# First tokens as rows turned by TensorE, head loads in one order, and a fixed table of order, engines and buffers in place of a list scheduler

## The chip, the cores and the metric

One core of a Trainium2 chip runs the kernel. The time is device microseconds of one execution, the median of several runs. A profiled execution has in addition a span, from the first to the last recorded instruction, and a trace of every engine. TensorE is called PE in the rows (PEld is its weight load), VectorE DVE, ScalarE ACT, GpSimd POOL; SP issues DMAs.

## The reference, cut to what matters

2048 tokens of width 640, 32 heads of 20. Branch A is a linear attention with learned feature maps, branch B a causal attention inside four segments of 512 tokens with a memory that is carried from segment to segment. A gate per token mixes them.

```python
q, k, v = A heads of x @ wqkv
phi_q = concat(softmax(q @ w_phi), softmax(-q @ w_phi))   # per head; phi_k alike
kv = sum over s of phi_k v ; z = sum over s of phi_k
a = (phi_q @ kv / (phi_q @ z + 1e-6)) @ wo_A
for s in range(4):                                       # branch B, L = 512
    p = softmax(qs @ ks.T * scale + causal mask)
    a_dot = p @ vs
    a_mem = phi(qs) @ M / (phi(qs) @ z + 1e-6)
    o = sigmoid(beta) * a_mem + (1 - sigmoid(beta)) * a_dot
    M += phi(ks).T @ vs ; z += sum phi(ks)
g = sigmoid((x * gate_w).sum(-1))
out = g * a + (1 - g) * (o @ wo_B)
```

## The kernel before, in words

The kernel is a graph of operations. Each method of `GatedMix` calls `op` or `dma` with the engines an operation may run on, a duration, the tiles it reads and writes, and a priority; an operation's place in this list of calls is its index. `schedule` (a list scheduler) then takes operation after operation by assumed durations and priorities: which comes next, which of two engines an evacuation runs on, which buffer of a pool and which PSUM banks a tile takes. `emit` writes one instruction stream per engine in that order, with a wait on a semaphore wherever an operand comes from another engine. On the chip every engine and every DMA queue takes its own stream in order.

PSUM has eight banks, handed out as single banks, pairs, or two pairs for a burst of QK. The exponentials of attention go to a pool `p_exp` of two buffers.

Names: `setup` loads. `x0` to `x3` are DMAs that turn 512 tokens each into `xT` (features on partitions); `stq`, `stk` are the q and k weights of branch B, which VectorE spreads into `WB` in groups of 32 columns; `WvB`, `WvA` the two v weights; `wkT`, `wqT` turned weights of branch A, from which `fuse` makes `WkA`, `WqA`. Segment n of branch B has ten `qkproj` (five chained 512-column matmuls, index 2c for q and 2c+1 for k of chunk c), four `vproj`, then eight steps in the order of GORD. A step (`b_step`) is three QK bursts (numbered 0, 1, 2), five exponentials of 128x1024 on ScalarE, four masks on GpSimd, two halves of PV (12 and 28 matmuls, numbered 0 and 1) and a combination of two VectorE operations. `Mmm`, `Nmm` update and read the memory; `b_out` scales and turns a tile into `oTB` by DMA. Branch A: `pkA`, `vA` for each of 16 token tiles, with a sum, a reciprocal, a product and running sums on VectorE; `kv` per segment; then `pqA`, `Zq`, a trip of the normaliser through DRAM, `U` per tile, turned into `oTA`. `final` adds both branches of one tile in 20 matmuls; its evacuation and the store to `out` follow. An evacuation (`evac`) may run on ScalarE or VectorE.

Before, SP issues x0, wkT, x1, x2, x3, wqT in this order, and ScalarE's queue stq, stk, WvB, WvA. The order of segments on TensorE, counted from one segment's first QK burst to the next, is in the table of the section on the change.

Of the kernel before, what the change touches and what calls it, by code (L numbers as in the profile page):

```python
# [13 lines left out]
D = 640  # L14
# [14 lines left out]
MW = 420 + 21 * 16  # L29

# [70 lines left out]
class Graph:  # L101
# [33 lines left out]
    def schedule(self):  # L135
        free = {s: 0.0 for s in STREAMS}
        bank_occ = [None] * 8
        bank_t = [0.0] * 8
        bank_prev = [()] * 8
        fillers = set()  # L140
        for o in self.ops:
            o.nleft = len(o.deps)
            for d in o.deps:
                d.succ.append(o)
            for t in o.tiles:
                t.left += 1
        ready = {s: [] for s in STREAMS}

        def push(o):
            for e in o.engs:  # L150
                ready[e].append(o)
        for o in self.ops:
            if o.nleft == 0:
                push(o)
        LAT = 0.09

        def dep_time(o, e):
            m = 0.0
            for d in o.deps:
                t = d.end  # L160
                if d.stream == e and e == "pe" and not d.dma:
                    continue
                if d.dma:
                    t = d.end + 0.1
                elif d.stream != e:
                    t += LAT
                else:
                    t += 0.03
                if t > m:
                    m = t  # L170
            return m

        def tile_avail(t, commit=False, rank=0):
            if t.slot is not None:
                return 0.0
            p = t.pool
            if p is None:
                return 0.0
            if isinstance(p, PsumPool):
                n = t.shape  # L180
                if n == 1:
                    best = None
                    for b in range(8):
                        if bank_occ[b] is None:
                            lone = bank_occ[b ^ 1] is None
                            c = (bank_t[b] + (0.3 if lone else 0.0), b)
                            if best is None or c < best:
                                best = c
                    if best is None:
                        return None  # L190
# [16 lines left out]
                if not opts:  # L207
                    return None
# [1034 lines left out]
```

## Time and profile before

| | us |
|---|---|
| median of 3 runs | 404.66 (404.42 to 407.14) |
| profiled execution | 401.42 |
| its span | 399.7 |
| TensorE busy | 313.9 |
| ScalarE busy | 257.3 |
| VectorE busy | 226.3 |
| GpSimd busy | 127.9 |

The profile has a page of totals, views of busy time by stretch, of groups of instructions by line, of instructions in order of time, of who waited for whom, and a chain of waits, followed back from the last instruction, which names at each moment the work that the end depended on. Busy times of different engines overlap. A matmul's recorded duration includes its way through the array, so chained matmuls follow each other faster than that.

### The profile page before, as it was taken

The page shows a single profiled execution, that of the slowest core. Times are in us where ns is not written, and L with a number is a line of the kernel's source. Part 1 is how long each engine was busy: PE and PEld are TensorE (multiplying, and loading weights), DVE is VectorE, ACT ScalarE, POOL GpSimd, SP SyncE. Part 2 cuts the span into 40 slices and gives each one's busy share as a digit, 9 for nine tenths or more (in the row PEclk, how much of TensorE's full clock was granted, in tenths as well). Part 3 has the DMA queues.
Part 4 walks back from the last instruction along what each step waited for, and adds up shares of the span by engine and source line. Part 5 has one row for each costly group of instructions (what it writes and reads, how often), then busy time and mean ns, then how long its engine had stood idle before and what let it go on. Part 6 is the DMA issues. An engine that isn't in the chain of part 4 may idle for free.

```text
span 399.7 us, 8357 instructions
## 1 busy us (share of the span) xinstructions
PE 313.9 (79%) x3594; PEld 180.9 (45%) x3594; DVE 226.3 (57%) x388; ACT 257.3 (64%) x334; POOL 127.9 (32%) x153
## 2 busy tenths in 40 slices
PE   0398796796888696988979689998999669938466
PEld 0144353463464354545326355554655346517233
DVE  3043696977797749658606996532443586126120
ACT  1047877579765855674977876797577864584602
POOL 5000561146535545272520232232322231133400
PEclk9999999899898969989989999999898857975559
DMA  8996800150100301006511526751320543423131
GB/s 184 301 202 115 128 15 16 30 77 2 52 18 2 66 2 31 13 16 195 66 48 28 134 48 150 147 85 46 59 59 16 115 98 80 130 84 36 32 66 66
DMA packets 70933, 30.51 MB, mean 76 GB/s; under 512 B 58961, under 2 KB 68465, under 8 KB 70897
## 3 DMA queue, kind: packets, MB, share of 16 engines
q1 hardware_dynamic: 68176, 26.68, 32.1%
q10 hardware_dynamic: 2624, 3.28, 2.6%
q0 software_dynamic: 96, 0.04, 0.5%
q8 instruction: 28, 0.46, 0.5%
q14 instruction: 9, 0.07, 0.1%
HBM read 10.08 MB, written 7.77 MB: 45 GB/s over the span
## 4 chain that ended last, share of the span: by engine, by line
PE 50%; DVE 25%; ACT 15%; DMA 5%; POOL 2%; issue 2%; POOLq 0%; ACTq 0%
PE ps L1162 9%; PE ps L736 9%; ACT expT L871 9%; PE ps L978 5%; PE ps L912 5%; DVE acc L1032 5%; PE ps L758 4%; DMA xT<-in_A_x_dram 4%; PE ps L1135 3%; PE ps L862 3%; PE ps L1083 3%; ACT expT L890 3%; DVE z L991 3%; DVE oA L1144 2%; PE ps L1163 2%
## 5 line engine op out<-in xcount | busy, mean ns | idle before, releaser
L876 POOL TENSOR_SCALAR_AFFINE_SELECT expT<-expT 128x512 bf16<-128x512 bf16 x128 | 92.5, 725 | 227.3 <-ACT expT L871 180.8
L871 ACT ACTIVATE expT<-ps 128x1024 bf16<-128x1024 f32 x128 | 124.0, 1025 | 30.9 <-PE ps L862 30.7
L736 PE MATMUL ps<-xT,WB 128*128 128x512 bf16 x200 | 51.2, 401 | 19.3 <-DMA xT<-in_A_x_dram 16.8
L912 PE MATMUL ps<-v1B,expT 128*128 128x21 bf16 x1280 | 40.7, 175 | 15.5 <-ACT expT L871 6.5
L912 PEld LDWEIGHTS ps<-v1B,expT 128*128 128x128 bf16 x1280 | 37.8, 98 | 25.5 <-POOL expT L876 8.5
L720 ACT ACTIVATE qkm<-ps 128x512 bf16<-128x512 f32 x31 | 18.4, 597 | 32.8 <-PE ps L736 32.6
L736 PEld LDWEIGHTS ps<-xT,WB 128*128 128x128 bf16 x200 | 19.0, 102 | 42.7 <-issue 22.4
L890 ACT ACTIVATE expT<-ps 128x1024 bf16<-128x1024 f32 x32 | 32.7, 1023 | 8.3 <-PE ps L862 8.2
L862 PE MATMUL ps<-qkm 20*128 20x512 bf16 (+3 forms) x320 | 23.3, 325 | 17.1 <-ACT expT L871 11.4
L1032 DVE TENSOR_TENSOR acc<-acc,E 64x1280 bf16<-64x1280 bf16 x31 | 32.9, 1061 | 5.9 <-POOL E L993 5.1
L993 POOL TENSOR_TENSOR E<-E,z 128x1280 bf16<-128x1280 bf16 x12 | 28.9, 2409 | 15.5 <-DVE z L992 15.5
L720 ACT ACTIVATE out<-ps 128x640 bf16<-128x640 f32 x16 | 11.3, 704 | 33.3 <-PE ps L1163 33.3
L758 PE MATMUL ps<-WvB,xT 128*128 128x512 bf16 x80 | 27.0, 419 | 4.0 <-DVE mo L952 1.2
L1162 PE MATMUL ps<-Wo,oTA 128*128 128x512 bf16 x80 | 24.9, 397 | 5.5 <-DMA oTB<-oB 4.4
L991 DVE TENSOR_REDUCE z<-E 128x64 f32<-128x1280 bf16 x16 | 23.7, 1479 | 9.3 <-ACT E L985 9.2
L985 ACT ACTIVATE E<-ps 128x640 bf16<-128x640 f32 x32 | 22.6, 707 | 9.1 <-PE ps L979 8.8
L978 PE MATMUL ps<-WkA,xT 128*128 128x512 bf16 x80 | 27.2, 426 | 1.0 <-DVE oB L921 1.0
L920 DVE RECIPROCAL cs<-ps 128x16 f32<-128x16 f32 x32 | 8.1, 252 | 34.9 <-PE ps L912 34.7
L978 PE MATMUL ps<-WvA,xT 128*128 128x512 bf16 x80 | 24.1, 386 | 2.8 <-DVE oB L921 2.0
L1083 PE MATMUL ps<-xT,WqA 128*128 128x512 bf16 x100 | 24.8, 388 | 0.4 <-DVE zf L1051 0.2
L1162 PE MATMUL ps<-Wo,oTB 128*128 128x512 bf16 x80 | 24.8, 395 | 0.0
L1088 ACT ACTIVATE ET<-ps 128x512 bf16<-128x512 f32 x40 | 23.2, 599 | 0.7 <-PE ps L1083 0.2
(114 smaller groups left out, 526.9 us busy)
## 6 DMA issues: line engine op xcount, KB each, us to landing
rx<-rc SPq DMA_DIRECT2D x16, 160.0 KB, 2.6
rr<-rx SPq DMA_DIRECT2D x4, 640.0 KB, 4.4
out_dram<-out SPq DMA_DIRECT2D x16, 160.0 KB, 2.0
scr<-qkm SPq DMA_DIRECT2D x16, 120.0 KB
qks<-scr SPq DMA_DIRECT2D x16, 120.0 KB
stq<-in_B_wq_dram ACTq DMA_DIRECT2D x1, 800.0 KB, 4.8
stk<-in_B_wk_dram ACTq DMA_DIRECT2D x1, 800.0 KB, 10.8
WvB<-in_B_wv_dram ACTq DMA_DIRECT2D x1, 800.0 KB, 12.9
```

Of the source, the lines that this page charges most:

```text
L736: r = e.matmul(self.pf(pt, 0, 0, LSEG), lhsT=self.WB[:, w, kc, 128 * c:128 * (c + 1)], rhs=xT[:, kc, LSEG * n:LSEG * (n + 1)], start=(kc = ...
L758: e.matmul(self.pf(pt, 0, 0, 512), lhsT=l, rhs=self.WvB[:, kc, 0:512], start=(kc == 0), stop=(kc == 4))
L862: r = e.matmul(self.pf(pt, i, c0, N), lhsT=view(32 * i, 32 * i + DH, 1, 128 * j, 128 * (j + 1)), rhs=view(32 * i, 32 * i + DH, 0, 128 * j, ...
L871: self.op("act", d_act(1024), lambda e, p=p: e.activation(ex[:, 2 * p:2 * p + 2, off:off + 512], self.pbanks(pt, 2 * p, 2, 512), ACT.Exp, ...
L876: self.op("pool", d_pool(n_el), lambda e: e.affine_select(view(), view(), pattern=pat, compare_op=ALU.is_ge, fill=0.0, base=0, channel_mul ...
L890: return e.activation(ex[:, :, 1024:1280].rearrange("p (k b) c -> p k b c", k=2), src, ACT.Exp, scale=scale)
L912: r = e.matmul(self.pf(ad, b, 256 * q2 + 21 * i, 21), lhsT=ex[:, i, c0:c0 + 128], rhs=vt[:, j, h, :], start=(j == 0), stop=(j == qi), skip ...
L978: e.matmul(self.pf(pt, 0, 0, 512), lhsT=l, rhs=W[:, kc, 0:512], start=(kc == 0), stop=(kc == 4))
L991: self.op("dve", 1.48, lambda e: e.tensor_reduce(z[:, :], Ev(), axis=AX.X, op=ALU.add), R=[(E, 0), (E, 1)], W=[(z, "*")], claim=[rz], pr=p ...
L1032: self.op("dve", 0.9, lambda e, src=src: e.tensor_tensor(acc[lo:lo + 64, :], acc[lo:lo + 64, :], src(), ALU.add), R=[(self.Et[t], 0), (sel ...
L1083: r = e.matmul(self.pf(pt, 0, 0, LSEG), lhsT=self.WqA[:, kc, 128 * c:128 * (c + 1)], rhs=xT[:, kc, LSEG * S:LSEG * (S + 1)], start=(kc == ...
L1162: e.matmul(self.pf(pt, 0, 0, 512), lhsT=l, rhs=self.Wo[:, c, 0:512], start=(c == 0), stop=(c == 9))
```

## The change

- `schedule` is replaced. ORDER lists the indices of all 1367 operations (base 36) in the order in which they are emitted; CHOICE has a digit for each of the 108 operations with two engines (0 the first named, 1 the second); WHERE a digit for every buffer or PSUM bank taken.
- The first 512 tokens are loaded as rows (`xk`, four DMAs of 160 KB into `xtok`, which lies on the first buffer of `p_exp`), turned by TensorE (`xtr`, five transposes of 128x128 per tile into one PSUM bank) and evacuated into `xT` (`xtr_ev`). `x0` falls away. Readers of the first segment's `xT` depend on single tiles (`xr`).
- `ident`, which the transposes need, is made first. The spread of `WB` is cut in two along the chunks (four operations more).
- Loads change queue and order. By the table SP issues: xk of tiles 2, 3, WvA, xk of tiles 0, 1, stk (after the landing of xk 2), WvB (after that of stq), x1, wkT, the small store of the head mask, wqT, then turned k chunks with x2 between them, and x3 behind the first segment's exchange of rows. ScalarE's queue issues only stq. GpSimd's queue issues beta, gate_w, w_phi after `ident`.
- TensorE's list begins: xtr 2, 0, 3, 1; vA 2, 3; qkproj 2, 0, 9, 1, 7; the first QK burst; vproj 0; qkproj 3; the second burst; qkproj 8; vproj 1; the third; qkproj 18 (the first of segment 1); ... It ends: the last bursts of steps 4 and 3 of the last segment with U 12 to 15, their PV, Nmm 10, and final 11, 10, 12, 15, 13, 14.
- Evacuations: 52 on ScalarE and 54 on VectorE (before, 71 and 31).

Operations on TensorE from the first QK burst (number 0) of a segment to that of the next, as the trace of before and the table have them; a column for the first segment stands under s0:

| | s0 before | after | s1 before | after | s2 before | after | s3 before | after |
|---|---|---|---|---|---|---|---|---|
| qkproj | 11 | 16 | 13 | 15 | 6 | 4 | 0 | 0 |
| vproj | 4 | 7 | 4 | 5 | 4 | 3 | 0 | 1 |
| pkA and vA | 20 | 16 | 12 | 14 | 0 | 0 | 0 | 0 |
| pqA | 0 | 0 | 10 | 9 | 7 | 7 | 3 | 4 |
| QK bursts | 24 | 25 | 24 | 23 | 24 | 24 | 24 | 24 |
| PV, halves | 16 | 14 | 14 | 16 | 18 | 16 | 16 | 18 |
| kv | 4 | 4 | 4 | 4 | 0 | 0 | 0 | 0 |
| fuse | 9 | 10 | 0 | 0 | 0 | 0 | 0 | 0 |
| Mmm, Zq, zmm | 1 | 1 | 3 | 3 | 3 | 3 | 1 | 1 |
| Nmm | 0 | 0 | 4 | 1 | 4 | 3 | 4 | 8 |
| U | 0 | 0 | 0 | 0 | 8 | 8 | 8 | 8 |
| final | 0 | 0 | 0 | 0 | 8 | 7 | 8 | 9 |

Ahead of s0 stand 10 qkproj, 4 vproj and one fuse before, and 4 xtr, 2 vA and 5 qkproj after. Of the finals of s3 the last four stand behind the last PV before, the last six after.

```diff
+ORDER = """
+4 0 1 g m 5 a 2 3 7 i n 6 8 o 1d 1f k qd b 1g j y l p ql qm 1e 2n 2o 1h 2j 1i 1k 1j 31 32 qe 2l 2m f 2k 2x 1o 3q 3s 2y 3r 3b 2p 3c h 11 3d 3u 2q 2z 3e
...
     def schedule(self):
-        free = {s: 0.0 for s in STREAMS}
...
+        order = [int(w, 36) for w in ORDER.split()]
+        choice = iter(CHOICE)
+        where = iter("".join(WHERE.split()))
         for o in self.ops:
...
+            o.stream = o.engs[0] if len(o.engs) == 1 else o.engs[int(next(choice))]
...
+        for i in order:
+            o = self.ops[i]
+            assert all(d in done for d in o.deps)
...
+                w = int(next(where), 36)
...
+            done.add(o)
+            self.order.append(o)
...
+        self.xtok = self.at("xtok", [128, 4, D], BF16, self.p_exp.slots[0].off)
+        self.overlay(self.p_exp, self.xtok)
...
-        for s in range(SEG):
+        xk = self.xtok
+        ld = [self.dma("sp", xk[:, tl, :], x2d[128 * tl:128 * (tl + 1), :], W=[(xk, tl)], pr=-60 + tl, name="xk", issue=0.4, lat=2.5 + 0.6 * tl) for tl in range(4)]
+        stq = self.dma("act", self.stq[:, :, :], wsrc(ins["B_wq"]), W=[(self.stq, "*")], pr=-50, name="stq", issue=0.45, lat=6.2)
+        stk = self.dma("sp", self.stk[:, :, :], wsrc(ins["B_wk"]), W=[(self.stk, "*")], pr=-50, name="stk", issue=0.5, lat=5.0, after=ld[2:3])
+        wvb = self.dma("sp", self.WvB[:, :, 0:D], wsrc(ins["B_wv"]), W=[(self.WvB, "w")], pr=-49, name="WvB", issue=0.5, lat=5.2, after=[stq])
+        wkt = self.dma("sp", self.wkT[:, :, :], wqkv[0:D, D:2 * D], W=[(self.wkT, "*")], pr=-48, transpose=True, name="wkT", issue=4.5, lat=2.5, after=[stk])
+        wva = self.dma("sp", self.WvA[:, :, :], wsrc(wqkv[:, 2 * D:3 * D]), W=[(self.WvA, "*")], pr=-47, name="WvA", issue=0.5, lat=4.8)
+        for s in range(1, SEG):
...
+        for tl in range(4):
+            pt = self.pst("xtr", 1)
+
+            def tr(e, tl=tl, pt=pt):
+                for c in range(NCH):
+                    r = e.transpose(self.pb(pt, 0, 128 * c, 128), xk[:, tl, 128 * c:128 * (c + 1)], self.ident[:, :])
+                return r
+            self.op("pe", 0.3, tr, R=[(xk, tl), (self.ident, "*")], W=[(pt, 0)], pr=-40 + tl, name="xtr")
+            self.evac(640, lambda tl=tl: xT[:, :, 128 * tl:128 * (tl + 1)], lambda pt=pt: self.pb(pt, 0, 0, 640).rearrange("p (c s) -> p c s", s=128),
+                      W=[(pt, 0), (xT, (0, tl))], pr=-40 + tl, name="xtr_ev")
...
+            for k0, k1 in ((0, 2), (2, 5)):
...
+    def xr(self, s, tl=None):
+        if s:
+            return [(self.xT, s)]
+        return [(self.xT, (0, k)) for k in (range(4) if tl is None else (tl,))]
```

## Rows read from the trace of the kernel before

**Rows 1.** Busy time by stretch: from:to us, length, busy of each engine, clock, DMA.

```profile
core 0: us, PE busy (x) PEld busy (x) DVE busy (x) ACT busy (x) POOL busy (x), PEclk, DMA share, GB/s
0.00:16.80 16.80, 0.03 (x1) 0.06 (x2) 3.68 (x12) 1.28 (x1) 5.03 (x12) 1.00 0.95 238
...
35.00:131.20 96.20, 78.16 (x922) 46.44 (x921) 76.24 (x107) 69.99 (x89) 42.79 (x40) 0.95 0.23 39
131.20:229.60 98.40, 79.72 (x868) 43.09 (x867) 65.34 (x98) 69.81 (x92) 37.38 (x38) 0.93 0.27 61
229.60:310.20 80.60, 75.43 (x954) 43.73 (x953) 39.34 (x84) 60.36 (x80) 21.42 (x32) 0.96 0.36 76
310.20:378.50 68.30, 48.63 (x691) 31.76 (x689) 32.76 (x69) 44.60 (x51) 21.27 (x32) 0.72 0.39 84
...
sum 399.70, PE 313.90 PEld 180.90 DVE 226.34 ACT 257.31 POOL 127.89; mean PE 44.84 PEld 25.84 DVE 32.33 ACT 36.76 POOL 18.27
```

**Rows 2.** Order of time on PE: start, length, line, op (first QK burst).

```profile
34.98 0.39 PE L862 MATMUL ps<-qkm 20*128 20x512 bf16 x4
```

**Rows 3.** Pieces of the chain of waits: start, length, engine, line.

```profile
175.53 0.86 PE ps L912 x28
...
186.24 1.41 PE ps L1009 x20
...
262.33 1.09 PE ps L1083 x5
263.42 0.33 PE ps L862 x8
...
355.81 0.92 ACT expT L890
356.73 2.76 ACT expT L871 x3
359.53 1.46 PE ps L1135 x12
```

**Rows 4.** The tail in order of time; brackets: idle before and what ended it.

```profile
380.29 5.16 SPq L602 DMA_TRANSPOSE oTB<-oB  x4
...
382.89 0.61 PE L1162 MATMUL ps<-Wo,oTA 128*128 128x512 bf16 x1 [4.40 <-DMA oTB<-oB]
...
393.95 0.70 ACT L720 ACTIVATE out<-ps 128x640 bf16<-128x640 f32 x1 [2.01 <-PE ps L1163]
396.66 0.70 ACT L720 ACTIVATE out<-ps 128x640 bf16<-128x640 f32 x1 [2.01 <-PE ps L1163]
```

**Rows 5.** The head in order of time, same columns.

```profile
0.81 4.90 SPq L602 DMA_TRANSPOSE xT<-in_A_x_dram  x1
...
5.63 1.19 DVE L664 COPY WB<-stq 128x2000 bf16<-128x2000 bf16 x1
...
5.77 12.33 SPq L602 DMA_TRANSPOSE wkT<-in_A_wqkv_dram  x1
...
16.77 8.11 PE L736 MATMUL ps<-xT,WB 128*128 128x512 bf16 x30 [16.77 <-DMA xT<-in_A_x_dram]
```

**Rows 6.** DMA issues: count, KB each, us from issue to landing.

```profile
stq<-in_B_wq_dram ACTq DMA_DIRECT2D x1, 800.0 KB, 4.8
...
WvA<-in_A_wqkv_dram ACTq DMA_DIRECT2D x1, 800.0 KB, 15.1
```

**Rows 7.** Groups by line: count | busy us, mean ns | idle before, releaser.

```profile
L720 ACT ACTIVATE qkm<-ps 128x512 bf16<-128x512 f32 x31 | 18.4, 597 | 32.8 <-PE ps L736 32.6
...
L720 ACT ACTIVATE v1B<-ps 128x640 bf16<-128x640 f32 x15 | 10.6, 707 | 0.4
L721 DVE CAST vA<-ps 128x640 bf16<-128x640 f32 x13 | 10.6, 816 | 10.6 <-PE ps L979 10.6
...
L721 DVE CAST qkm<-ps 128x512 bf16<-128x512 f32 x9 | 6.1, 688 | 30.6 <-PE ps L736 30.6
```

**Rows 8.** Who waited for whom: us in total, times, longest.

```profile
PEld ps L862 <- ACT expT L871: 22.0, 17, 2.3
```

More of the change, by code (lines that the diff above doesn't have):

```diff
@@ new lines, in schedule @@
+        bank = [None] * 8
+        done = set()
+        self.order = []
+        assert sorted(order) == list(range(len(self.ops)))
+        for i in order:
+            o = self.ops[i]
+            assert all(d in done for d in o.deps)
+            for t in dict.fromkeys(list(o.claim) + o.tiles):
+                if t.slot is not None or t.pool is None:
+                    continue
+                w = int(next(where), 36)
+                if isinstance(t.pool, PsumPool):
+                    if t.shape == 1:
+                        t.slot = [w]
+                    elif t.shape == 2:
+                        t.slot = [2 * w, 2 * w + 1]
+                    else:
+                        t.slot = [2 * (w // 4), 2 * (w // 4) + 1, 2 * (w % 4), 2 * (w % 4) + 1]
+                    t.t = t.slot
+                    t.prev = [d for b in t.slot if bank[b] is not None for d in bank[b].ops]
+                    for b in t.slot:
+                        assert bank[b] is None or bank[b].left == 0
+                        bank[b] = t
+                else:
+                    s = t.pool.slots[w]
+                    assert all(x.left == 0 for x in s.occ)
+                    t.slot = s
+                    t.prev = [d for x in s.occ for d in x.ops]
+                    s.occ = [t]
+                    self.alloc(t)
@@ L332, in schedule @@
             for t in o.tiles:
                 t.left -= 1
-                if t.left == 0 and isinstance(t.pool, PsumPool):
-                    fillers.discard(t)
-                    for b in t.slot:
-                        bank_occ[b] = None
-                        bank_t[b] = max(d.end for d in t.ops)
-                        bank_prev[b] = tuple(t.ops)
-            for u in o.succ:
-                u.nleft -= 1
-                if u.nleft == 0:
-                    push(u)
-        self.makespan = max(o.end for o in self.order)
@@ L346 @@
-    MAXPAIRS = 2
-    def filler_ok(self, fillers, t):
-        pairs = set()
-        for f in fillers:
-            for b in f.slot:
-                pairs.add(b // 2)
-        if t.shape == 1:
-            for p in pairs:
-                pass
-            return len(pairs) <= self.MAXPAIRS
-        return len(pairs) < self.MAXPAIRS
-    def dump(self, ready, est, bank_occ):
-        print("STUCK; banks", [t.name if t else None for t in bank_occ])
-        for e in STREAMS:
-            for o in ready[e]:
-                bad = [t.name for t in list(o.claim) + o.tiles if t.slot is None and t.pool is not None]
-                print(e, o.name, o.pr, bad)
+            done.add(o)
@@ L628, in setup @@
[L628 to L630 removed]
+        op = self.op
+        idt = self.ident
@@ L981, in mmf @@
             return mm
[L982 removed]
+        self.op("pe", d_mm(*[512, 128] * 5), mmf(pt, self.WkA), R=[(self.WkA, ic) for ic in range(NCH)] + self.xr(S, t % 4), W=[(pt, 0), (pt, 1)],
                 claim=[E], pr=pr, name="pkA")
```

260 lines of the change are left out of this document (52 added, 208 removed).

## The prediction, made before the changed kernel ran

> **What bounds the kernel now.** I read the page first, then the busy time by stage, the prices of single pieces in the chain of waits, the head and the tail in order of time, and the groups by line. In a span of 399.7 us TensorE is busy for 313.9, ScalarE for 257.3 and VectorE for 226.3 [rows 1]. No engine is full, so the reader should ask when TensorE, the busiest, stands still. The view by stage cuts the span at the first QK burst of each of the four segments (35.0 [rows 2], and likewise 131.2, 229.6 and 310.2 us) and at the end of the last PV (378.5). In the first 16.8 us TensorE does nothing. To put a figure on the four segments I price TensorE's work at the full rate: five chained 512-column matmuls take 1.09 us, a PV half of 28 matmuls 0.86, a kv of 20 at most 1.41, a QK burst 0.25 to 0.40 (0.33 in the row) [rows 3]. Four outputs are evacuated 2.71 us apart, which is the price of a `final`; the ten matmuls of a vproj, pkA or vA are half of one, 1.36, and 1.40 with the step to the next [rows 4]. The smaller pieces are priced from their steps in the same chain (the short PV half 0.47, U 0.8, Nmm 0.6, Mmm 1.8, Zq 1.2, fuse 0.5). Times the counts of the segments (the table ahead of this) that is 75.9, 75.9, 74.8 and 54.1 us of work. The first three segments last 96.2, 98.4 and 80.6 us: TensorE's work fills 0.79, 0.77 and 0.93 of them. The fourth lasts 68.3 us to the last PV, and without the four finals behind it (10.9) holds 43.2 us of work: 0.63. In that stretch the mean granted clock is 0.72, so more than half of it runs at 1.2 GHz and not at 2.4 [rows 1]. Neither TensorE nor ScalarE (44.6 of 68.3 us busy) is full there; the chain of waits goes from one to the other, as from ScalarE's exponentials to a U on TensorE [rows 3]. So the kernel is bound by the order in which four in-order engines meet, and the change rewrites just that.
>
> **The head.** Before, the first projection starts at 16.77 us, released by the turned load of the first tokens, whose issue took 4.90 us from 0.81 and whose data came 11 us after that [rows 5], among four weight loads of 800 KB. The change loads those tokens as rows (160 KB each) and puts them, WvA and the two projection weights into one queue, in an order. TensorE's order starts with the 20 transposes and then vA of tiles 2 and 3, so the first projection waits for all four row loads and WvA. Next to them only stq is under way: 4 x 160 + 2 x 800 KB are 2.29 MB, at the 238 GB/s of the stretch [rows 1] 9.6 us, plus the 0.8 at which the first issue stands [rows 5]: 10.4. A landing bound from below is stq's 4.8 us from issue, from above WvA's own 15.1 [rows 6]; with its issue a microsecond behind the first the first projection lies between 6.6 and 16.9, and I take 10.5.
>
> The transposes are not in the trace. The nearest row is a 128-column matmul: half a `final` (1.36) less five of 512 (1.09) leaves 0.27 for five, 0.054 each at the full clock and double that at half: 1.1 to 2.2 us for twenty. They run while TensorE waits for WvA; without that cover they cost the 2.2. Their four evacuations (0.7 to 0.8 us each by the 640-column ones [rows 7]) fall on engines that idle there (VectorE 3.68 us busy of 16.8 [rows 1]). The splitting of the four weight spreads into eight adds four short instructions on VectorE, in the same idle time; the spread of 2000 columns takes 1.19 us [rows 5] and the q weights are there by the time two vA are done. The Trainium skill, page "VectorE: DVE Perf Modes", section "The three transpose paths", gives 390 ns for a 128x128 transpose on TensorE; by it twenty would be 7.8 us, those of the last tile 1.4 us more than by the rows, and the forecast 369 instead of 368.
>
> Then come two vA (2.8) and five qkproj (5.4), 8.2 us, and the clock ramp: the first 30 matmuls before took 8.11 us [rows 5] where 30 x 0.218 are 6.5, so 1.6 more. First QK burst: 10.5 + 8.2 + 1.6 = 20.3 us instead of 35.0. Part of this is only work put off (16.9 us of TensorE work stood before the first QK, now 9.6 with the transposes).
>
> What the moved loads pass: SP now issues stk behind the wait for the first row load and WvB behind the wait for stq, and the turned loads of x1, wkT and then wqT stand behind both. stq, 4.8 us from its issue before [rows 6], should be in by 7.5 among more row loads; x1 issued then, and taking as long as x0 did (15.8), lands at 23.3, and its first reader (qkproj 18) comes 6 us after the first QK, at 26. For wkT the issue before took 12.33 us [rows 5]; 7.5 + 0.5 + 4.9 + 12.3 is 25 and landing 29, while its first reader stands near 31. Both are covered, with 2 to 3 us to spare; if the cover is gone, TensorE waits there once for what is over. wqT stands also behind the store of the head mask, which VectorE now begins after the evacuation of qkproj 5, near 27 us: with the masks, 3.6 of issue and some 6 to landing it is there near 37, its reader near 36; a microsecond may go there.
>
> **The middle.** No arithmetic leaves the kernel. By the new choices 52 evacuations are ScalarE's (71 before) and 54 VectorE's (31), three of the new ones being turned tokens. At 597 against 688 ns for 512 columns and 707 against 816 for 640 [rows 7] ScalarE falls by 12 us to about 245, VectorE rises by 17 to about 243; both stay under TensorE. The work per segment, priced as above, becomes 79.3, 80.4, 66.5 and 46.7 us (the last without the six finals that now end the list), VectorE's by the same order 65, 77, 48 and about 45, ScalarE's 66, 65, 55 and 46.
>
> How well the segments fill is the unknown of this sum. Its bounds: no better than before (0.79, 0.77, 0.93, 0.63), or everywhere as the third segment already is, 0.93. In the first segment VectorE stood at 77 us against TensorE's 76, and the chain runs through it for long stretches; now it has 65 against 79, so it leaves slack. In the fourth, before, four finals (10.9 us) and all of the last normaliser stand inside one attention step while the steps behind it have 2 to 4 us of TensorE work against 4.6 of exponentials (five at 0.92 [rows 3]); now these steps are interleaved with U, Nmm and two finals. For both I go half of the way: 0.86 and 0.78. In the second segment VectorE's 77 stand against 80, no slack, so a quarter of the way: 0.81. The third keeps 0.93. That gives 92.2 + 99.3 + 71.5 + 59.9 us.
>
> **The tail.** Before, TensorE waits 4.40 us for oTB, then runs four finals, the first at half clock (382.89 to about 388.2, 5.3 instead of 2.7) [rows 4]. Now finals 11 and 10, whose inputs are long there, stand between the last PV and the four: 5.4 us, more than the wait. Six finals are 16.3 us and what follows the last is 3.1 (396.6 to 399.7): 19.4. What it buys is the wait and the clock, some 7 us.
>
> **Sum.** 20.3 + 92.2 + 99.3 + 71.5 + 59.9 + 19.4 = 362.6 us of span, against 399.7. The profiled execution took 401.42 with 1.7 us around its span, 3.2 less than the median 404.66 of the three runs; with both, 362.6 + 1.7 + 3.2 = 367.5, so 368.
>
> **The rivals.** *Only the head and the tail gain.* The waits in the middle come from the dependences (exponential, mask, PV, combination with two exp buffers), not from the order, and the segments fill as before: 20.3 + 100.4 + 104.4 + 71.5 + 74.1 + 19.4 = 390.1, so 395. For it: 22.0 us of TensorE's waits for a QK burst are for ScalarE to free PSUM [rows 8], and neither the two buffers nor the eight banks change. Against it: the third segment has the same buffers and fills to 0.93.
>
> *The middle becomes dense.* All four at 0.93: 20.3 + 293.4 + 19.4 = 333.1, so 338. Against it: VectorE would be 89% busy in the second segment, and no stretch in the trace shows that.
>
> *The head gains nothing.* WvA, now needed first, lands as late as before, the first projection starts at 17.5, and all of TensorE's order stands behind it: 7 us more, 375. For it: bulk loads that overlap all landed late before (stq alone in 4.8, WvA in 15.1 [rows 6]). Against it: fewer bytes are asked for ahead of it. The Trainium skill, page "DMA: Bandwidth & Descriptors", section "Issuing engines are not separate DMA queues", says that transfers from several issuing engines interleave on the same sixteen DMA engines; by it stq and stk share with WvA whichever queue they are in, and only bytes and order count. The landings before agree with it.
>
> *The new order stalls, and it is slower.* The table fixes the order inside each engine; QK bursts now come second, third, first in places, PV halves turned round, and an engine whose next instruction is late holds all behind it. The price is a QK burst that waits for ScalarE: 22.0 us over 17 times, 1.3 us [rows 8]. From the forecast, 25 more of the 96 bursts that wait so bring it to 400.6, the edge of no change, and 32 more to 408.7, slower. For it: 17 such waits already, and engines fuller than before leave less to catch up with. Against it: the order before was fixed at build time just the same.
>
> **How the numbers follow.** The forecast 0.54 (352 to 385 by its own bounds: 0.04 of filling either way in the first, second and fourth segments is some 12 us, the head 4 to 6), only head and tail 0.16, head gains nothing 0.11, dense 0.08, stalls 0.11. The likeliest time is 368. A range of 345 to 395 leaves out most of the stalls, most of the dense case and part of the first rival, about 2 in 10. A measurement of this kernel can tell about 1% from no change: faster is under 400.6, slower over 408.7. The stalls and the upper end of the first rival give 0.07 for the same and 0.06 for slower; the rest, 0.87, is faster.
>
> **What would show it.** After: the first matmul of vA near 10.5, the first QK burst near 20 (35.0 before), the last stretches' granted clock above 0.8, no wait for oTB ahead of the last finals, ScalarE near 245 and VectorE near 243 us, TensorE busy no more than before. Wrong would be: a first projection after 16 us; a wait of TensorE for x1 or wkT; segments that fill under 0.8 again with long rows of TensorE waiting for VectorE; a fourth segment still at a clock near 0.7.

## The result, and the profile after

The changed kernel takes 350.99 us (median of 4 runs, 350.18 to 354.26) against 405.9 us for the kernel before, run beside it (median of 4): a ratio of 0.866 with a 95% interval of 0.859 to 0.873, faster by some 55 us. The profiled execution took 350.18 us, with a span of 348.1. Some executions of a kernel come out 1 to 3% longer at a lower granted clock; the ratios leave these out, the medians here and below count all.

First the busy time by stretch, cut like [rows 1] at the first query-key burst of each segment (22.8, 108.7, 198.4 and 268.3 us) and at the end of the last PV (328.8); the columns are those of [rows 1].

```profile
core 0: us, PE busy (x) PEld busy (x) DVE busy (x) ACT busy (x) POOL busy (x), PEclk, DMA share, GB/s
0.00:13.10 13.10, 2.25 (x20) 2.02 (x21) 2.92 (x7) 1.56 (x2) 2.92 (x8) 1.00 0.86 244
13.10:22.80 9.70, 9.70 (x48) 4.48 (x45) 4.01 (x9) 2.93 (x6) 0.00 (x0) 1.00 0.99 231
22.80:108.60 85.80, 78.35 (x903) 45.18 (x902) 65.24 (x93) 67.71 (x87) 41.25 (x43) 0.98 0.35 63
108.60:198.40 89.80, 81.92 (x906) 45.40 (x904) 76.29 (x115) 67.39 (x93) 42.56 (x39) 0.96 0.26 60
198.40:268.20 69.80, 65.71 (x864) 38.86 (x860) 44.50 (x94) 56.87 (x72) 18.62 (x30) 0.98 0.44 85
268.20:328.80 60.60, 49.85 (x767) 32.03 (x766) 38.56 (x87) 45.39 (x53) 22.22 (x35) 0.83 0.44 105
328.80:348.10 19.30, 16.26 (x120) 9.06 (x118) 5.56 (x13) 3.30 (x5) 0.00 (x0) 0.98 0.48 108
sum 348.10, PE 304.04 PEld 177.03 DVE 237.07 ACT 245.16 POOL 127.56; mean PE 43.43 PEld 25.29 DVE 33.87 ACT 35.02 POOL 18.22
```

Of the 51.6 us by which the span falls, TensorE stands still for 41.7 less (399.7 - 313.9 = 85.8 before, 348.1 - 304.0 = 44.1 after), and its busy time falls by the other 9.9, with a higher granted clock in every segment (most in the fourth, 0.72 to 0.83). The head, up to the first burst, is 12.2 us shorter, the four segments 10.4, 8.6, 10.8 and 7.7, the tail some 2.

Second, where TensorE's waits went. The line is the share of the span by engine in the chain that ended last; first before, then after.

```profile
PE 50%; DVE 25%; ACT 15%; DMA 5%; POOL 2%; issue 2%; POOLq 0%; ACTq 0%
```

```profile
PE 53%; DVE 22%; DMA 9%; ACT 9%; SPq 3%; issue 2%; POOL 1%; POOLq 0%
```

ScalarE's share falls from 15% of 399.7 us (60) to 9% of 348.1 (31), VectorE's from 25% (100) to 22% (77); DMA's rises from 5% (20) to 9% (31). ScalarE's is the largest movement. A share of the chain is a rough measure (kernels as fast as this one will show 11 and 13% for ScalarE below), but the waits agree: added up by engine, the waits of TensorE's matmuls (line for line, without those of the weight loads) go from 35.3 to 9.2 us for ScalarE and from 21.9 to 18.0 for VectorE. The row that answers to [rows 8], waits ahead of a query-key burst for the exponentials, halves; there are as many waits, each shorter:

```profile
PEld ps L733 <- ACT expT L742: 11.1, 19, 1.2
```

Third, the head in order of time (start, length, engine, line, operation; in brackets the idle time before it and what ended it), answering to [rows 5].

```profile
2.19 1.10 SPq L458 DMA_DIRECT2D xtok<-in_A_x_dram  x2
...
6.36 10.23 SPq L454 DMA_TRANSPOSE xT<-in_A_x_dram  x1
...
11.54 1.78 PE L493 MATMUL ps<-ident,xtok 128*128 128x128 bf16 x15 [7.10 <-DMA xtok<-in_A_x_dram]
13.11 0.63 PE L849 MATMUL ps<-WvA,xT 128*128 128x512 bf16 x1
...
16.64 3.85 SPq L454 DMA_TRANSPOSE wkT<-in_A_wqkv_dram  x1
...
22.81 0.40 PE L733 MATMUL ps<-qkm 20*128 20x512 bf16 x4
```

The first tile of tokens, number 2, is turned at 3.75 us. Next in TensorE's order is tile 0, whose row load stands behind WvA on SP's queue: issued at 2.19 with that of tile 1, 160 KB each, it lands at 11.5. All three remaining tiles stand still until then, 7.10 us.

### The profile page after: what moved, and what is told of

It reads as the page before. It is cut to its first block, busy times and chain, and to the rows that moved or that the text cites. A ratio compares the mean times of both kernels' runs of the same rounds, so it can differ in the third digit from the quotient of the medians.

```text
span 348.1 us, 8430 instructions
## 1 busy us (share of the span) xinstructions
PE 304.0 (87%) x3614; PEld 177.0 (51%) x3614; DVE 237.1 (68%) x415; ACT 245.2 (70%) x315; POOL 127.6 (37%) x153
## 4 chain that ended last, share of the span: by engine, by line
PE 53%; DVE 22%; DMA 9%; ACT 9%; SPq 3%; issue 2%; POOL 1%; POOLq 0%
PE ps L607 9%; PE ps L1033 8%; PE ps L849 6%; PE ps L783 5%; PE ps L733 5%; ACT expT L742 5%; DVE acc L903 5%; PE ps L1006 4%; PE ps L629 3%; DMA rr<-rx 3%; DMA xtok<-in_A_x_dram 3%; PE ps L954 3%; DVE z L862 2%; PE ps L1034 2%; PE ps L880 2%
## 5 line engine op out<-in xcount | busy, mean ns | idle before, releaser
L747 POOL TENSOR_SCALAR_AFFINE_SELECT expT<-expT 128x512 bf16<-128x512 bf16 x128 | 91.1, 727 | 158.0 <-ACT expT L742 107.0
L607 PE MATMUL ps<-xT,WB 128*128 128x512 bf16 x200 | 48.0, 380 | 0.0
L783 PE MATMUL ps<-v1B,expT 128*128 128x21 bf16 x1280 | 38.6, 173 | 5.7 <-DVE KVZacc L891 2.0
L783 PEld LDWEIGHTS ps<-v1B,expT 128*128 128x128 bf16 x1280 | 35.9, 97 | 13.2 <-POOL expT L747 7.5
L587 DVE CAST qkm<-ps 128x512 bf16<-128x512 f32 x21 | 14.3, 682 | 17.5 <-PE ps L607 17.5
L629 PE MATMUL ps<-WvB,xT 128*128 128x512 bf16 x80 | 23.9, 381 | 1.4 <-DVE vA L587 1.3
L849 PE MATMUL ps<-WkA,xT 128*128 128x512 bf16 x80 | 24.5, 395 | 0.6 <-ACT E L856 0.4
L856 ACT ACTIVATE E<-ps 128x640 bf16<-128x640 f32 x32 | 22.3, 708 | 1.9 <-PE ps L850 1.4
L1033 PE MATMUL ps<-Wo,oTB 128*128 128x512 bf16 x80 | 23.4, 379 | 0.0
L586 ACT ACTIVATE out<-ps 128x640 bf16<-128x640 f32 x12 | 8.2, 704 | 19.1 <-PE ps L1034 19.1
L1006 PE MATMUL ps<-K,ET 128*128 128x147 bf16 (+1 forms) x192 | 17.6, 262 | 2.8 <-DVE ET L991 2.5
```

The source lines that it names most:

```text
L607: r = e.matmul(self.pf(pt, 0, 0, LSEG), lhsT=self.WB[:, w, kc, 128 * c:128 * (c + 1)], rhs=xT[:, kc, LSEG * n:LSEG * (n + 1)], start=(kc = ...
L629: e.matmul(self.pf(pt, 0, 0, 512), lhsT=l, rhs=self.WvB[:, kc, 0:512], start=(kc == 0), stop=(kc == 4))
L747: self.op("pool", d_pool(n_el), lambda e: e.affine_select(view(), view(), pattern=pat, compare_op=ALU.is_ge, fill=0.0, base=0, channel_mul ...
L783: r = e.matmul(self.pf(ad, b, 256 * q2 + 21 * i, 21), lhsT=ex[:, i, c0:c0 + 128], rhs=vt[:, j, h, :], start=(j == 0), stop=(j == qi), skip ...
L849: e.matmul(self.pf(pt, 0, 0, 512), lhsT=l, rhs=W[:, kc, 0:512], start=(kc == 0), stop=(kc == 4))
L1006: r = e.matmul(self.pf(pt, f, 21 * (h0 - 16 * f), 21 * (h1 - h0 + 1)), lhsT=ET[:, c, s, 128 * tl:128 * (tl + 1)], rhs=K1[:, s, c, h0 - HB[ ...
```

## The experiments

The order of work, the choice of engine and the choice of PSUM bank stand in three tables, `ORDER`, `CHOICE` and `WHERE`, so each could be changed alone. No run leaves out any of the computation. The table gives the first query-key burst of each segment (read from TensorE's instructions in order of time) and the four lengths that follow from them; "rest" is the last segment and the tail, up to the end of the span of the profiled execution.

| kernel | median us | first burst | s0 | s1 | s2 | rest |
|---|---|---|---|---|---|---|
| before | 405.9 | 35.0 | 96.2 | 98.4 | 80.6 | 89.5 |
| changed | 351.0 | 22.8 | 85.9 | 89.8 | 69.8 | 79.8 |
| eA: new head, list order | 402.9 | 34.5 | 98.2 | 99.1 | 79.7 | 90.2 |
| eD: old head, table | 357.1 | 27.3 | 85.4 | 89.9 | 70.2 | 82.3 |
| eC: table, list's engines | 385.3 | 25.3 | 94.5 | 102.4 | 79.0 | 83.6 |
| eK: table, engines exchanged | 376.9 | 25.0 | 94.4 | 97.9 | 78.4 | 78.1 |
| eF: table, other banks | 375.7 | 22.8 | 90.7 | 92.0 | 77.9 | 91.6 |
| eI: VectorE +11.8 us in s0 | 358.8 | 22.3 | 95.9 | 88.5 | 68.8 | 80.8 |
| eJ: VectorE +11.8 us in s1 | 356.0 | 22.4 | 86.8 | 98.4 | 68.9 | 78.1 |

**Head, engines and order, apart.** Four kernels cut the change along its parts.

*eA*, the new `setup` under the old list scheduler:

```diff
-        order = [int(w, 36) for w in ORDER.split()]
-        choice = iter(CHOICE)
...
+        free = {s: 0.0 for s in STREAMS}
+        bank_occ = [None] * 8
```

> The new first loads, the turning of the first tokens by TensorE and the load order of the changed kernel, but order, engines and buffers of everything by the old list scheduler. Theory 'order' (the table's order of the long middle carries most of the gain): only the head is gained, the first query-key burst comes some 10 us earlier than before, the four stretches stay as thinly filled as before, 390 to 399 us. Theory 'head' (an early first burst lets ScalarE start early, and the rest follows by itself): 355 to 370 us, and the second and third stretch fill to 0.9.

Measured: 402.88 us (397.85 to 405.4), ratio to before 0.990 [0.973, 1.007], not to be told from no change, and above what either theory gave. Its first projection starts at 12.49 us instead of 16.77, but the list scheduler still puts all ten qkproj of the first segment, with other work on the first tokens, ahead of the first burst, which stays at 34.5. An earlier start that nothing in the order uses is worth almost nothing; the theory "head" falls, and of "order" the part that the first burst would come 10 us sooner.

*eB*, the same with the table's engines:

```diff
+        choice = iter(CHOICE)
+        for o in self.ops:
+            if len(o.engs) > 1:
+                o.engs = (o.engs[int(next(choice))],)
```

> The kernel eA_list_newhead with one thing more: where an operation may go to either of two engines, it goes to the one that the table names; the order and the buffers are still the list scheduler's. Theory 'order': within 6 us of eA_list_newhead, either way. Theory 'engines' (ScalarE is relieved, its busy time falls from 264 to about 245 us, and this is what the second and third stretch gain from): 355 to 375 us.

Measured: 406.03 us (401.96 to 409.17), ratio 1.001 [0.995, 1.006]. ScalarE's busy time did fall to 246.6 us, as in the changed kernel, and it bought nothing: relieving ScalarE is not, by itself, the gain.

*eC*, the other way round, the table's order and banks with the list's engines (52 of 108 choices):

```diff
-CHOICE = "111001010110110101010110000111110000010110110111101010111100000011111100101111111000101000011000110000000100"
+CHOICE = "111011101100110010000000000000000110000000000000000000101111001010000011111111001101110100010000000000000000"
```

> The changed kernel with its order and its buffers, but 52 of its 108 choices of engine set back to what the list scheduler chose before (those that evacuate the turned tokens stay). Theory 'order': at most 8 us over the changed kernel, 350 to 359 us. Theory 'engines': 368 to 385 us, with ScalarE's busy time back at about 264 us and waits of TensorE for exponentials in the second and third stretch.

Measured: 385.31 us (384.86 to 386.49), ratio 0.954 [0.946, 0.962]: 34 us over the changed kernel. That is close to the number of "engines", and not that of "order". Yet ScalarE has only 255.9 us of work here, 11 more than in the changed kernel, and VectorE 222.4, 15 less. So either 11 us more on ScalarE cost 34, or the order doesn't suit other engines; eK below speaks for the second.

*eD*, the old loads and turning with the table for the rest:

```diff
-        for s in range(1, SEG):
+        for s in range(SEG):
...
-        for tl in range(4):
-            pt = self.pst("xtr", 1)
```

> The old setup and loads (first tokens turned by the DMA, the loads of before on their queues of before), and from there on order, engines and buffers of the table. Theory 'order': the first burst comes 8 to 12 us later than in the changed kernel, the rest is as dense, 357 to 364 us. Theory 'head': 385 to 400 us.

Measured: 357.08 us (356.9 to 358.19), ratio 0.884 [0.877, 0.892]. The segments are as in the changed kernel (85.4, 89.9, 70.2). TensorE waits for WvA until 17.7 us, 4.6 us later than the changed kernel's first projection, and the burst comes 4.5 us later; the end comes 6.1 us later. So under the table the new head is worth 6 us, and under the list scheduler 3 that can't be told from nothing; the table without the new head is worth 49. (Part of the 6 us is a mismatch: the old loads bring WvA last, and the table's order needs it first.)

**Load or match.** *eK* exchanges the engines within 31 pairs of neighbouring operations of the same kind. Each engine keeps its load.

```diff
-CHOICE = "111001010110110101010110000111110000010110110111101010111100000011111100101111111000101000011000110000000100"
+CHOICE = "111011001011011001001011001010001111101001001110110101110100110100111101010111101101000100100011000100010000"
```

> The changed kernel, order and buffers of the table, but in 31 pairs of neighbouring operations of the same kind (62 of the 108 choices) the two engines are exchanged: the first goes to the engine of the second and the other way round. Each engine keeps its number of operations of each kind, so ScalarE's and VectorE's busy times stay at 245 and 237 us, within 2. Theory 'load' (in eC_table_list_engines it was ScalarE's 11 us more work that cost 34 us): 349 to 357 us. Theory 'match' (the table's order is worth its time only with the engine that each operation was given, since a swap puts an evacuation behind another instruction of an in-order engine): 362 to 385 us.

Measured: 376.94 us (375.93 to 378.21), ratio 0.933 [0.927, 0.939]: 26 us lost with nothing done but exchanges between neighbours. "Match" stands and "load" falls. The chain of eK, by engine:

```profile
PE 44%; DVE 24%; ACT 18%; DMA 6%; issue 3%; POOL 2%; SPq 1%; POOLq 0%
```

ScalarE has 18% of 373.9 us, 67, against 31 in the changed kernel, though its work is the same. The reading that fits is that evacuations now stand ahead of exponentials, or behind them, where the order did not mean them to be; no single exchange was followed through. What the trace shows is the waits: those of TensorE's matmuls for ScalarE add up to 17.9 us (9.2 in the changed kernel) and for VectorE to 27.2 (18.0).

**Banks.** *eF* leaves order and engines and gives 226 of 310 PSUM tiles another bank. One of the four changed lines:

```diff
-01230213021361217261b010b03123063112313123140b01012132023210312003167231136231201b2400b30b163201632060331610306302402361013631603002333603103600630216
+01230213010321b03b206670673612760612060201243102010112323220017003201732130231211b1410b02b32323112206033161010b302402271013631603002331b01103b00b0121b
```

> The changed kernel, with order and engines of the table, but the PSUM banks given out anew, always those that have been free longest: 226 of 310 tiles in another bank. Theory 'order and engines': within 4 us of the changed kernel, 348 to 355 us. Theory 'buffers' (the table's choice of banks is a part of the gain of its own): 358 us or more.

Measured: 375.72 us (374.39 to 377.11), ratio 0.928 [0.921, 0.936]: 25 us. "Buffers" holds. In the program a tile waits for the readers of the tile that had its bank before, so the bank decides for whom it waits, even in an unchanged order. The chain of eF by engine, and its last two stretches:

```profile
PE 56%; DVE 16%; ACT 16%; DMA 5%; POOL 2%; issue 2%; SPq 1%
```

```profile
205.53:283.43 77.90, 66.70 (x863) 38.92 (x861) 44.44 (x94) 57.45 (x72) 19.54 (x31) 0.96 0.37 75
283.43:375.00 91.57, 71.55 (x886) 43.17 (x884) 44.07 (x99) 48.64 (x58) 22.11 (x35) 0.79 0.38 92
```

Again it is ScalarE in the chain (16% of 375.0 us, 60), TensorE's matmuls wait 23.8 us for it, and most of the loss is in the last two segments, where the granted clock over the last stretch is 0.79. In part the loss may be due to the rule used here (longest free in the order); how the list's own rule would do under the table's order was not tried.

**Does VectorE's slack set the filling?** The prediction let the second segment gain little because VectorE would be nearly full there. *eI* issues the sum over E (1.48 us on VectorE) twice for the first eight token tiles, *eJ* for the last eight.

```diff
+        def zred(e):
+            if t < 8:
+                e.tensor_reduce(self.zx[:, t % 8, :], Ev(), axis=AX.X, op=ALU.add)
+            return e.tensor_reduce(z[:, :], Ev(), axis=AX.X, op=ALU.add)
```

> The changed kernel, with the sum over E (1.48 us on VectorE) issued twice for the first eight token tiles, the extra result unused: 8 x 1.48 = 11.8 us more work for VectorE, nearly all of it in the first stretch (22.8 to 108.6 us, VectorE busy 65.2 of 85.8 us). Theory 'slack' (a stretch gets slower only when VectorE has no slack left in it): +0 to +3 us. Theory 'chain' (each VectorE step stands in a chain from evacuation to the next matmul, with or without slack): +6 to +12 us.

> The same extra sum over E for the last eight token tiles: 11.8 us more for VectorE, most of it in the second stretch (108.6 to 198.4 us), where VectorE is busy 76.3 of 89.8 us and would come to about 88. Theory 'slack': the second stretch grows by 6 to 11 us, the total too. Theory 'chain': the same growth as in eI_vector_load_s0, 6 to 12 us for both. Theory 'TensorE alone sets the stretch': under 2 us for both.

Measured: eI 358.76 us (358.01 to 361.98), ratio 0.895 [0.886, 0.903], 7.8 us over the changed kernel; eJ 356.01 us (355.62 to 357.07), ratio 0.887 [0.878, 0.895], 5.0 us over it. The loaded stretch of each, eI's first and eJ's second:

```profile
22.27:118.14 95.87, 80.41 (x903) 45.59 (x903) 73.58 (x101) 68.01 (x87) 40.07 (x43) 0.96 0.31 56
```

```profile
109.15:207.53 98.38, 84.60 (x907) 46.43 (x906) 84.92 (x122) 67.53 (x93) 41.10 (x38) 0.93 0.24 55
```

The stretch with 20 us of slack on VectorE (65.24 of 85.80 busy) grew by 10.0 us, the one with 13.5 by 8.6. All eight extra sums of eI lie in its first stretch (11.8 us), seven of the eight of eJ in its second (10.3 us), so they cost 0.85 and 0.83 of their length. "Slack" falls: more slack did not make the work cheaper. "Chain" fits, as the sum stands in the chain that ended last (in eI the extra sums alone, `DVE zx`, are 3.2% of 356.3 us there, 11.4 us). Later stretches made up some of it, and eJ's total of 5.0 us lies below what either of the two theories gave. VectorE work that stands in no such chain was not tried.

**The tail.** *eE* puts the finals 11 and 10 behind the last four: of the tail of `ORDER`, 11k, 11l, 11m (matmuls, evacuation and store of tile 11) and 11h, 11i, 11j (tile 10) go to the end, their entries in `WHERE` with them (one of the others takes another buffer).

```diff
-10g or ot 109 ou 10b o6 10i 10a o7 10c oy oz o8 jw lb o9 jx oe 10j of og oh 10l 10k pg 10m 11d ph oi p0 p1 oj ok ol pi 11k 11h p6 p7 pd pj 10h p8 11n
-pk pe pf pr ps pt pl 11o 11w 11x pm 11i 11q 11l 11m 11r 11s 11y 11j 11p 11t 11u 11v
+od 10d os 107 10e 108 10f 10g or ot 109 ou 10b o6 10i 10a o7 10c oy oz o8 jw lb o9 jx oe 10j of og oh 10l 10k pg 10m 11d ph oi p0
+p1 oj ok ol pi p6 p7 pd pj 10h p8 11n pk pe pf pr ps pt pl 11o 11w 11x pm 11q 11r 11s 11y 11p 11t 11u 11v 11k 11l 11m 11h 11i 11j
```

> The changed kernel, but the last matmul groups of output tiles 11 and 10 stand behind those of the four last tiles and not in front of them. By the prediction they cover the wait for the last turned normalised outputs: without them TensorE waits 4 to 5 us between the last PV and the finals, runs the first of them at the lower clock, and the total grows by 4 to 7 us, 355 to 358 us. If nothing needs that cover: within 1 us of the changed kernel.

Measured: 353.95 us (352.31 to 357.68), ratio 0.874 [0.867, 0.882]. The total is 3.0 us over the changed kernel in the medians, but the intervals of the two ratios overlap, so it can't be told from no loss. The trace of the tail tells: the wait is back, as long as in [rows 4], and the first final behind it steps 0.51 us from one pair of matmuls to the next, where the changed kernel's step is 0.27. First the changed kernel around its last PV, then eE behind its own:

```profile
327.88 0.86 PE L783 MATMUL ps<-v1B,expT 128*128 128x21 bf16 x28 [0.24 <-POOL expT L747]
328.60 0.38 PE L1033 MATMUL ps<-Wo,oTA 128*128 128x512 bf16 x1
...
328.87 0.38 PE L1033 MATMUL ps<-Wo,oTA 128*128 128x512 bf16 x1
```

```profile
326.19 0.86 PE L791 MATMUL ps<-v1B,expT 128*128 128x21 bf16 x28 [0.24 <-POOL expT L755]
331.53 0.61 PE L1041 MATMUL ps<-Wo,oTA 128*128 128x512 bf16 x1 [4.48 <-DMA oTB<-oB]
331.93 0.31 PE L1042 MATMUL ps<-Wo,oTA 128*128 128x128 bf16 x1
332.04 0.63 PE L1041 MATMUL ps<-Wo,oTA 128*128 128x512 bf16 x1
```

From the end of the last PV to the end of the span eE takes 26.05 us (327.05 to 353.1) and the changed kernel 19.36 (328.74 to 348.1): 6.7 us more, for the same six finals. In eE's profiled execution what lies ahead happened to be 1.7 us shorter, so the spans differ by 5.0.

**Can the head give more?** *eG* moves only WvA behind the four row loads on SP:

```diff
-4 0 1 g m 5 a 2 3 7 i n 6 8 o 1d 1f k qd b 1g j y l p ql qm 1e 2n 2o 1h 2j 1i 1k 1j 31 32 qe 2l 2m f 2k 2x 1o 3q 3s 2y 3r 3b 2p 3c h 11 3d 3u 2q 2z 3e
+4 0 1 g m 5 2 3 a 7 i n 6 8 o 1d 1f k qd b 1g j y l p ql qm 1e 2n 2o 1h 2j 1i 1k 1j 31 32 qe 2l 2m f 2k 2x 1o 3q 3s 2y 3r 3b 2p 3c h 11 3d 3u 2q 2z 3e
```

> The changed kernel with one load moved: the value weights' first half leaves SP after the four row loads of tokens, not between the second and the third. Theory 'ring' (a small load lands late when a large one stands ahead of it on its queue): the third and fourth row load land at about 5 us and not at 11.5, the transposes end by about 8 us, the first projection then waits for the value weights, and starts at 10.5 to 12 us; total -1 to -2.5 us. Theory 'bandwidth' (all that is loaded in the head shares one rate, order matters little): first projection at 13 us as now, total within 0.5 us.

```profile
7.88 1.78 PE L493 MATMUL ps<-ident,xtok 128*128 128x128 bf16 x15 [3.26 <-DMA xtok<-in_A_x_dram]
12.20 0.59 PE L849 MATMUL ps<-WvA,xT 128*128 128x512 bf16 x1 [2.54 <-DMA WvA<-in_A_wqkv_dram]
```

Measured: 349.71 us (349.43 to 350.96), ratio 0.871 [0.865, 0.878]. Both theories are half right: the last row loads are in 3.7 us sooner (7.88 against 11.54), though not at 5, and now WvA is what is waited for, only 0.9 us sooner than the first projection of the changed kernel (12.20 against 13.11). The total is 1.3 us lower, within the spread of the runs, and the ratio is no lower (0.871 against 0.866).

*eH* also issues stk ahead of WvA and moves five projections and the burst ahead of the two vA; the beginning of `ORDER` (the first digits of `WHERE` change places with it):

```diff
-4 0 1 g m 5 a 2 3 7 i n 6 8 o 1d 1f k qd b 1g j y l p ql qm 1e 2n 2o 1h 2j 1i 1k 1j 31 32 qe 2l 2m f 2k 2x 1o 3q 3s 2y 3r 3b 2p 3c h 11 3d 3u 2q 2z 3e
+4 0 1 g m 5 2 3 7 a i n 6 8 o k b j l p 1d 1f 1g 1e 2n 2o 2j 2k 1h 1i 1k 1j y 2l 2m 31 32 2x
```

> As eG_rows_first, with the key statistics' weights ahead of the value weights as well, and on TensorE the five projections that feed the first scores and the first query-key burst ahead of the two value projections of the first tokens. If what opens the second stretch is when ScalarE gets its first exponentials: the first burst at 14 to 17 us in place of 22.8, total -3 to -6 us. If the work of TensorE in the first stretch, and not the exponentials, sets the time from there on (the two value projections have only changed places with the burst): within 1.5 us of eG_rows_first.

Measured: 350.8 us (349.24 to 351.82), ratio 0.873 [0.866, 0.880], as eG within the spread. The burst came at 18.89, later than hoped and still 3.9 us sooner than in the changed kernel, and was worth nothing in the total. TensorE in order of time, then busy times and granted clock from the burst to 30 us:

```profile
18.89 0.39 PE L741 MATMUL ps<-qkm 20*128 20x512 bf16 x4
21.33 0.39 PE L857 MATMUL ps<-WvA,xT 128*128 128x512 bf16 x1 [2.05 <-ACT expT L750]
...
22.09 0.63 PE L857 MATMUL ps<-WvA,xT 128*128 128x512 bf16 x1
22.51 0.31 PE L858 MATMUL ps<-WvA,xT 128*128 128x128 bf16 x1
22.62 0.63 PE L857 MATMUL ps<-WvA,xT 128*128 128x512 bf16 x1
```

```profile
18.89:30.00 11.11, 9.06 (x56) 4.24 (x56) 2.38 (x5) 4.77 (x7) 0.00 (x0) 0.85 0.34 74
```

The vA behind the burst waits 2.05 us for ScalarE's exponentials; the first pair of matmuls after that stop steps 0.29 us, the next seven 0.44 to 0.54 instead of 0.27, at a granted clock of 0.50 from 22 to 25 us (0.85 over the whole row). By 25.7 us eH has done what the changed kernel has done by 23.1 (five projections, the burst, two vA): it is 2.6 us behind in work, and its total is still the same. The total is what the second theory gave, but its reason, that TensorE's work sets the time from there on, would have these 2.6 us cost something. Why neither the early burst nor the late work moves the total stays open; the early burst without this stop was not tried.

*eL* fills the wait of eG for WvA with three q projections, whose data are in (`WHERE` again in step):

```diff
-4 0 1 g m 5 a 2 3 7 i n 6 8 o 1d 1f k qd b 1g j y l p ql qm 1e 2n 2o 1h 2j 1i 1k 1j 31 32 qe 2l 2m f 2k 2x 1o 3q 3s 2y 3r 3b 2p 3c h 11 3d 3u 2q 2z 3e
+4 0 1 g m 5 2 3 a 7 i n 6 8 o 1d 1f 1g 1e k b j p l 2n 2o 2j 2k y 2z 30 ql qm qd 1h 1i 1k 1j
```

> The load order of eG_rows_first, and the time in which TensorE there waits for the value weights (9.7 to 12.2 us) filled with work whose data are in: the query projections 2, 0 and 8, then the two value projections of the first tokens, then the key projections 9, 1 and 7 and the first query-key burst; everything behind that as in the changed kernel. In eH_qk_first the burst came 3.9 us earlier than in the changed kernel and the total did not move. Theory 'work' (that was because the same TensorE work was left to do, and the burst's place alone is worth nothing): here 2.5 us of idle time are filled, one more projection is done ahead of the burst, which starts at 20 to 21 us, and the total falls by 2 to 4 us against eG_rows_first, 346 to 348 us. Theory 'absorbed' (what is gained ahead of the first burst is lost again in the waits of the first stretch, whatever its kind): within 1 us of eG_rows_first, 349 to 351 us.

Measured: 350.22 us (348.1 to 353.6), ratio 0.876 [0.869, 0.883]. In the profiled execution the burst comes at 21.02, 1.8 us sooner than in the changed kernel, and the span is 346.0, 2.1 us shorter; over the runs that is within the spread. The median is what "absorbed" gave, but the spread takes in what "work" gave too. Whether eG or eL is faster than the changed kernel by a microsecond or two stays open; none of the three heads beats it by what can be measured.

## Why the prediction was right, and where not

The verdict was right and the time, 351, lies in the range, 17 us under the forecast. In terms of its own sum (span, us):

| term | predicted | measured | error |
|---|---|---|---|
| head | 20.3 | 22.8 | +2.5 |
| first segment | 92.2 | 85.8 | -6.4 |
| second | 99.3 | 89.8 | -9.5 |
| third | 71.5 | 69.8 | -1.7 |
| fourth | 59.9 | 60.6 | +0.7 |
| tail | 19.4 | 19.3 | -0.1 |
| span to median | 4.9 | 2.9 | -2.0 |

**The filling of the first and second segment: the step that failed.** Together they were forecast 15.9 us too long, which is nearly the whole error. Priced as in the prediction, TensorE's work fills 79.3/85.8 = 0.92 and 80.4/89.8 = 0.90 of them, not 0.86 and 0.81; the third has 0.95, the fourth 0.77 (forecast 0.78). "Half of the way" was a guess that missed in the first segment and hit in the fourth, so the hit is luck and not a sign that the rule is good. The reason given for going only a quarter of the way in the second, no slack left on VectorE, was wrong: VectorE is busy for 76.29 of its 89.80 us, 85%, and the stretch is dense. eI and eJ say why such a reason doesn't hold here: added VectorE work cost 0.85 of its length where there was much slack and 0.83 where there was less. VectorE's busy share does not tell what a stretch loses to it; that where its instructions stand in the chain does is what fits, shown for this one sum alone. The rival of a dense middle (0.93 in all four) was nearly right for three segments, and I gave it 0.08.

**The order as the gain: right, with a limit.** That the waits lay in the order and not in the dependences is borne out by eD against eA: 49 us with the table and the old head, 3, not clear of the noise, with the new head and the old order. But "order" was too narrow a word. The table's order with other engines loses 34 us of the 55 (eC), with neighbours exchanged 26 (eK), with other banks 25 (eF): the three don't add up, as each has its worth only with the others. The text counted the engines by their loads (ScalarE 245, VectorE 243; measured 245.16 and 237.07) and the banks not at all. What all three broken kernels share in the trace is TensorE's matmuls waiting for ScalarE again: 23.3 us in eC, 17.9 in eK and 23.8 in eF, against 9.2 in the changed kernel and 35.3 before. In the chain ScalarE has 16 to 21% there, against 9% (eC's chain follows). The chain alone would not show it: eG and eL, as fast as the changed kernel, have 11 and 13% (10.2 and 11.7 us of waits), and eA, no faster than before, has 11% (33.7 us of waits). Which misplaced evacuation costs how much was not taken apart.

```profile
PE 47%; ACT 21%; DVE 20%; DMA 6%; issue 4%; POOL 1%; SPq 1%; POOLq 0%; ACTq 0%
```

**The head.** From the first projection to the first burst it was right (8.2 + 1.6 = 9.8 predicted, 9.7 measured), and so was that wkT and x1 are covered: TensorE waits for neither. But that was in part luck, as two wrong prices met: wkT's issue took 3.85 us instead of the 12.33 that I counted, x1's 10.23 instead of 4.90. The first projection was wrong, 13.11 us instead of 10.5, in two steps. The row loads landed 1.0 us late, at 11.5: up to then 228 GB/s were moved, 2.62 MB, where the sum had 2.29. It left out that SP would go on to issue stk (at 3.63, as the first row load was in by then), WvB (5.94) and x1 (6.36); no run takes these loads away, so their share is worked out and not shown. The Trainium skill, page "DMA: Bandwidth & Descriptors", section "Issuing engines are not separate DMA queues", puts it that transfers from several issuing engines interleave on the same sixteen DMA engines; these 2.62 MB agree. The other 1.6 us are the transposes (next paragraph). And the 14.7 us by which the head gets shorter are not all gain, since the 7.3 us of work put off (16.9 less 9.6) come back in the segments, where the sum did count them: eD puts the new head at 6 us.

**The transposes.** Twenty took 0.69 + 1.78 = 2.47 us, a little over the upper bound of 2.2. The cover that I named, the wait for WvA, wasn't there, as the row loads were what TensorE waited for, and the 15 behind them delayed the first projection by 1.6 us. In eG the cover is there: TensorE waits 2.54 us for WvA behind them. The Trainium skill, page "VectorE: DVE Perf Modes", section "The three transpose paths", has 390 ns for one; 15 in 1.78 us are 0.12 us each, and the measurement decides.

**The fourth segment and the tail: right.** No wait for oTB stands ahead of the last finals, the granted clock is 0.83 and 0.98 in the last two stretches. What the cover buys was put at some 7 us; taken away in eE the tail gets 6.7 us longer in the trace, the total 3.0 in the medians, which is not clear of the noise.

**From the span to the median.** I added 3.2 us, the distance of the one profiled execution of before to its median. After, that distance is 0.8. It was a matter of chance in one execution, and belonged into the range.

**The rivals.** That only head and tail gain is refuted by the segments, 10.4, 8.6, 10.8 and 7.7 us shorter, and by eD, which has their gain without the new head. That the order stalls is refuted too: TensorE waits for the exponentials ahead of a QK burst for 11.1 us over 19 times, against the 22.0 over 17 of [rows 8]. That the head gains nothing had WvA land as late as before and the first projection at 17.5 us; it came at 13.11, though in the total the head gains little. eC, eK and eF show that the mechanism of a stalling order is real: TensorE's matmuls wait 57.2 us for ScalarE and VectorE before, 27.2 in the changed kernel, and 52.7, 45.1 and 44.5 in these three.

## What to carry to other kernels

Order, engine and buffer of an operation are one decision where in-order engines meet: take over a found schedule whole, and after any edit to one part of it search again, since here 31 exchanges between neighbours, with equal loads, cost 7%. Judge a stage by what stands in its chain of waits, not by how busy its engines are: here sums of 1.5 us each on an engine that was busy three quarters of the time cost some 85% of their length. An earlier start is worth only what the order behind it can use; check it against the first work that is released, not against the clock.

## What the runs showed of the hardware

After standing still TensorE can step at half pace for a while. In the tail of eE and in eH the granted clock shows it (0.50 from 22 to 25 us in eH, and 0.50 from 331.5 to 335.6 in eE). In the head it does not: from 13.10 to 22.80 us the row says 1.00, and yet the first vA steps 0.53 us from one pair of matmuls to the next (13.11, 13.64), and the second, for the most part, 0.27 (16.51, 16.78).

```profile
13.11 0.63 PE L849 MATMUL ps<-WvA,xT 128*128 128x512 bf16 x1
13.54 0.31 PE L850 MATMUL ps<-WvA,xT 128*128 128x128 bf16 x1
13.64 0.63 PE L849 MATMUL ps<-WvA,xT 128*128 128x512 bf16 x1
...
16.51 0.38 PE L849 MATMUL ps<-WvA,xT 128*128 128x512 bf16 x1
16.72 0.22 PE L850 MATMUL ps<-WvA,xT 128*128 128x128 bf16 x1
16.78 0.38 PE L849 MATMUL ps<-WvA,xT 128*128 128x512 bf16 x1
```

And a small load takes the place that its queue gives it: the same 160 KB row load was in by 11.5 us behind an 800 KB load of its queue and by 7.9 ahead of it.
